# An RWKV block on one core: the bonus term of two groups moved to a ones-block matmul and a channel-major v, and xr's preparation queued behind k's evictions

## The chip, the cores and the metric

The kernel runs on 1 core of one Trainium2 chip, as one program. The metric is device time in microseconds, the median of several runs. Engines: PE is TensorE, DVE is VectorE, ACT is ScalarE, POOL is GpSimd, and SP is the engine that issues most DMAs.

## The reference

Three layers follow one another, for B=2 sequences of S=768 tokens, 8 heads of D=48 channels (384 in all):

```
for t in range(S):                                   # layer 1: linear attention
    cur = einsum('bhd,bhe->bhde', u[None] * kt, vt)  # the bonus of the current token
    y[:, :, t] = einsum('bhd,bhde->bhe', rt, state + cur)
    state = wt[..., None] * state + einsum('bhd,bhe->bhde', kt, vt)
xk = mu_k * x + (1 - mu_k) * x_prev                  # layer 2: x is y, x_prev the token before
xr = mu_r * x + (1 - mu_r) * x_prev
x2 = sigmoid(xr @ w_r) * (relu(xk @ w_k)**2 @ w_v)
h = gelu(x2 @ w_in); u, v = halves of h              # layer 3: gated unit mixing over tokens
out = x2 + (u * (w_sg @ norm(v) + b_sg)) @ w_out
```

The bonus adds, for one token, (sum over d of r_d u_d k_d) times v_e to y_e: one scalar for each token and head, times the head's v.

## The kernel before, in words

Tokens are cut into four groups of 384 (two per sequence), each group into three chunks of 128. The eight heads go in pairs, so a group has four *units* of one pair each, and there are 16 units, 0 to 15. A pair lies on 112 partitions: head 0 on 0 to 47, head 1 on 64 to 111.

A unit runs in four steps. `attn_prep` (DVE) makes decay products by scans, the scaled keys `kp`, the scaled queries `rp`, and `ruk` = r u k. `attn_sc` (step S, line 345) transposes `kp` into PSUM (`kt_ps`, line 351), sums `ruk` over channels by matmuls with the two-column `hm` into the same PSUM tile (`bs`, line 354), has ACT copy the transposed keys out (`kt`, line 357), and forms the scores (`sc`, line 365). DVE then forms `vb` = v times the bonus sums (line 369, v being token-major) and masks the scores (`am`, line 374). `attn_kv` (step K) makes the chunk states. `attn_y` (step Y) collects y for the pair in one PSUM tile: scores times v (line 424), `vb` times the identity (line 427), states times `rp` (line 430); ACT evicts it to `yo` (line 435), and SP copies `yo` by DMA to its place in `xx` (line 444).

Layer 2 runs by group in steps k (8 tiles of 128 rows of `w_k`), r (3) and v (3, each in four parts). `moe1_prep` makes its operand xk or xr from `xx`: for each of three row blocks ACT scales (`dx`, line 484), DVE mixes in the shifted tokens (line 487), and where products are split into a high and a low half, ACT copies the high half (line 490) and DVE subtracts (line 491). A k tile is evicted by ACT (`kr`, line 510). Most products are split: three matmuls in a short fp32 format (`fp32r`) stand for one. The first steps use plain fp32 instead, one matmul that the trace records as two.

The order of PE's instructions is written out by hand: a list of steps in which the attention steps of the next group are woven between the k, r and v steps of the present one, so that units 4 to 7 run beside group 1's layer 2, units 8 to 11 beside group 2's and 12 to 15 beside group 3's. Group 4's layer 2 and then layer 3 follow without attention. The other engines and their DMA queues are ordered by a planner: each operation has a due time (`at(...)`, from the planned start `TS` or end `TE` of a step), and the planner takes, among what is ready in its own model, what is due first. On the chip each queue then runs in that fixed order. `tc.issue_after(ins)` adds that the operations of the block on `ins`'s engine stand behind `ins` in that queue. Tiles of one tag share `bufs` buffers; a new tile waits until the oldest one's readers are done.

xr of group 1 to 4 is prepared once the first k tile of the group has been issued (`if kd == "k" and key[2] == 0`), with due times just ahead of the r step.

Weights come in 64-bit words and are converted on chip (`load64`, lines 225 to 229); a tile tag `wl` with NW1 + SPARE buffers holds full weights, low halves, and pieces of layer 3's weights that are converted ahead.

Of the kernel before, what the change touches and what calls it, by code (L numbers as in the profile page):

```python
# [4 lines left out]
F32 = mybir.dt.float32  # L5
# [3 lines left out]
AF = mybir.ActivationFunctionType  # L9
ALU = mybir.AluOpType  # L10
PSUM = bass.MemoryType.PSUM

B, H, S, D = 2, 8, 768, 48
DM, DFF, DH = 384, 1024, 512
CH = 128
G = 384
GB = S // G
NG = B * GB
CG = G // CH
NP = H // 2  # L20
PW = 2 * D
HP = 64
PR = HP + D
# [5 lines left out]
KS = S // 128  # L29
NTOK = B * S  # L30
NW1 = 2 * KF + KM
SPARE = 4
ND0 = 22
ND = 1
B_STG = 3
# [3 lines left out]
T_GAP = 4.5  # L39
T_TAIL = 9.0  # L40
VQ = 4
L_SPLIT = 2
L_CV = 12
L_CK = 6
# [15 lines left out]
def emit(tc, tin, nin, vt, consts, ucp, mu_k, mu_r, g_ln, b_sg, w_k, w_v, w_r, w_in, w_sgT, w_out, outT):  # L60
# [87 lines left out]
    pl = {"w": tc.alloc_tile_pool(name="pw", bufs=1, side="left", reuse_waits="tile")}  # L148
    pa = tc.alloc_tile_pool(name="pa", bufs=2, side="right", reuse_waits="tile")

    cst = pa.tile([128, 128 + 128 + 2], F32, name="cst", bufs=1)
    ident = cst[:, 0:128]
    cmask = cst[:, 128:256]
    hm = cst[0:PR, 256:258]
    d1f = pa.tile([PR, WL], F32, name="d1f", bufs=1)
    u_sb = pa.tile([PR, NP], F32, name="u_sb", bufs=1)
    flag = cp.tile([1, 1], I32, name="flag")
# [20 lines left out]
    for t in sblk[0] + sblk[1] + scar:  # L178
        PL.memset(t, 0.0)

    uw, urk, uv = {}, {}, {}

    def load_t(i):
        s, hp = divmod(i, NP)
        g, c0, n = subs[s]
        src = tin[g * NP + hp]
        wl = n * (CH + 1) + 1
        w = pa.tile([PR, wl], F32, name="uw", tag="uw", bufs=3)
        rk = pa.tile([PR, 2, n * CH], F32, name="urk", tag="urk", bufs=3)
        e = A if i < 2 else SP  # L190
        with at(TS["S", i] - 9 if i >= 2 else -19.9 + 0.25 * i):
            SP.dma_start(w, src[:, c0 * (CH + 1):c0 * (CH + 1) + wl])
        with at(TS["S", i] - 8.5 if i >= 2 else -19.8 + 0.2 * i):
            e.dma_start(rk, src[:, WL:WL + 2 * G].rearrange("p (q t) -> p q t", q=2)[:, :, c0 * CH:(c0 + n) * CH])
        uw[i], urk[i] = w, rk

    def load_n(i):
# [147 lines left out]
    def attn_sc(i):  # L345
        tS, tK, tY = TS["S", i], TS["K", i], TS["Y", i]
        s = st[i]
        nc_ = subs[i // NP][2]
        kt_ps = pq.tile([128, 512], F32, name="kt_ps", tag="kt", bufs=1)
        for c in range(nc_):  # L350
            PE.transpose(kt_ps[:, c * PR:(c + 1) * PR], s["kp"][:, c], ident[0:PR, 0:PR])
        bs = kt_ps[:, nc_ * PR:nc_ * PR + 2 * nc_]
        for c in range(nc_):
            PE.matmul(bs[:, 2 * c:2 * c + 2], s["ruk"][:, c * CH:(c + 1) * CH], hm, start=True, stop=True)  # L354
        kt = pa.tile([128, nc_, PR], F32, name="kt", tag="ktsb")
        with at(tS + 0.5):
            A.activation(kt, kt_ps[:, 0:nc_ * PR].rearrange("p (c d) -> p c d", d=PR), AF.Copy)
        s["kt"] = kt
        am = pa.tile([128, 2, nc_, CH], F32, name="am", tag="am", bufs=B_AM)
        sc = [pq.tile([128, 512], F32, name="sc", tag="sc", bufs=2)[:, 0:nc_ * CH].rearrange("p (c t) -> p c t", t=CH)  # L360
              for _ in range(2)]
        for c in range(nc_):
            for h in range(2):
                hs = slice(h * HP, h * HP + D)
                PE.matmul(sc[h][:, c], s["kp"][hs, c], s["rp"][hs, c], start=True, stop=True)  # L365
        vb = pa.tile([128, nc_, 2, D], F32, name="vb", tag="vb", bufs=2)
        with at(tY - 1.4):
            bh = bs.rearrange("p (c h) -> p c h", h=2)[:, :, :, None].to_broadcast([128, nc_, 2, D])
            V.tensor_tensor(vb, uv[i].rearrange("p c (h d) -> p c h d", h=2)[:, :, :, 0:D], bh, ALU.mult)
        s["vb"] = vb  # L370
        for h in range(2):
            with at(tY - 1.2 + 0.4 * h):
                mask = cmask[:, None, :].to_broadcast([128, nc_, CH])
                V.tensor_tensor(am[:, h], sc[h], mask, ALU.mult)  # L374
        s["at"] = am
# [39 lines left out]
    def attn_y(i):  # L415
        s = st[i]
        si, hp = divmod(i, NP)
        g, c0, nc_ = subs[si]
        y = pq.tile([128, 512], F32, name="y", tag="y", bufs=1)
        y3 = y[:, 0:nc_ * CH].rearrange("p (c t) -> p c t", t=CH)  # L420
        for c in range(nc_):
            for h in range(2):
                hs = slice(h * HP, (h + 1) * HP if h == 0 else PR)
                PE.matmul(y3[hs, c], uv[i][:, c, hs], s["at"][:, h, c], start=(c == 0), stop=False, skip_group_check=True)  # L424
        for c in range(nc_):
            for h in range(2):
                PE.matmul(y3[h * HP:h * HP + D, c], s["vb"][:, c, h], ident, start=False, stop=False, skip_group_check=True)  # L427
        cs = [c for c in range(nc_) if s["us"][c] is not None]
        for c in cs:
            PE.matmul(y3[0:PR, c], s["us"][c], s["rp"][:, c], start=False, stop=(c == cs[-1]), skip_group_check=True)  # L430
        yo = pa.tile([PR, nc_ * CH], F32, name="yo", tag="yo", bufs=2)
        if hp == 0 and g % GB == 0 and c0 == 0:
            PL.memset(xx[g][:, :, 0:1], 0.0)
        with at(TE["Y", i] - 0.3):
            A.activation(yo, y[0:PR, 0:nc_ * CH], AF.Copy)
        with at(TE["Y", i] - 0.2):
            for h in range(2):
                a = hp * PW + h * D
                e = a + D
                while a < e:  # L440
                    j, p = divmod(a, 128)
                    n = min(e - a, 128 - p)
                    q = h * HP + a - hp * PW - h * D
                    SP.dma_start(xx[g][p:p + n, j, 1 + c0 * CH:1 + (c0 + nc_) * CH], yo[q:q + n])
                    a += n
        if hp == NP - 1 and c0 + nc_ == CG and g % GB != GB - 1:
            with at(TE["Y", i] + 2):
                PL.tensor_copy(xx[g + 1][:, :, 0:1], xx[g][:, :, G:G + 1])
# [20 lines left out]

    m1 = {}  # L470

    def moe1_prep(s, which):
        g, c0, n = subs[s]
        t0, t1 = c0 * CH, (c0 + n) * CH
        x = xx[g]
        mu, nu, nm = ((mk_sb, nk_sb, "xk"), (mr_sb, nr_sb, "xr"))[which]
        nat = is_nat(s, "kr"[which])
        ops = tuple(pl["w"].tile([128, KM, t1 - t0], F32 if nat else F32R, name=nm + q, tag=nm + q, bufs=1)
                    for q in ("h" if nat else "hl"))
        dl = TS[("k", "r")[which], s, 0] - (4 if s == 0 and which == 0 else 0)  # L480
        for j in range(KM):
            d = pl["w"].tile([128, t1 - t0], F32, name="dx", tag="dx", bufs=2)
            with at(dl - 2.5 + 0.5 * j):
                A.activation(d, x[:, j, 1 + t0:1 + t1], AF.Copy, scale=mu[:, j:j + 1])  # L484
            o = ops[0][:, j] if nat else d
            with at(dl - 2 + 0.5 * j):
                last = V.scalar_tensor_tensor(o, x[:, j, t0:t1], nu[:, j:j + 1], d, ALU.mult, ALU.add)  # L487
                if nat:
                    continue
                A.activation(ops[0][:, j], d, AF.Copy)  # L490
                V.tensor_tensor(ops[1][:, j], d, ops[0][:, j].bitcast(F32), ALU.subtract)
        m1[s, which] = ops
        return last

# [8 lines left out]
    def moe1_k(s, f):  # L503
        nat, nt = is_nat(s, "k"), subs[s][2] * CH
        ps = mm_tile()[:, 0:nt]
        mm(ps, [(part(wt["k", f], slice(None), j), part(m1[s, 0], slice(None), j)) for j in range(KM)])
        kr = pl["w"].tile([128, nt], F32, name="kr", tag="kr", bufs=2)
        te, tv = TE["k", s, f], TS["v", s, 0] + f * MM[s, "v"]
        with at(te):
            A.activation(kr, ps, AF.Relu)  # L510
        vn = is_nat(s, "v") and (f < NVN or not split_ops[0])
        kh = pl["w"].tile([128, nt], F32 if vn else F32R, name="kh", tag="kh", bufs=KF)
        dl = min(te + 1, tv - 2)
        if s == NAT["k"] - 1:
            split1("k", f, TS["k", s + 1, f])
        if vn:
            with at(dl):
                A.activation(kh, kr, AF.Square)
            m1[s, "k", f] = (kh,)
            return  # L520
        kl = pl["w"].tile([128, nt], F32R, name="kl", tag="kl", bufs=KF)
        with at(dl):
            A.activation(kh, kr, AF.Square)
            A.activation(kr, kr, AF.Square)  # L524
            V.tensor_tensor(kl, kr, kh.bitcast(F32), ALU.subtract)  # L525
        m1[s, "k", f] = (kh, kl)
# [252 lines left out]
    for n, key in enumerate(keys[:n_in]):  # L779
# [4 lines left out]
        if kd == "Y":  # L784
# [7 lines left out]
            prep(g + 2)  # L792
            if g % NP == NP - 1:
                moe1_prep(g // NP, 0)
        if kd == "k" and key[2] == 0:
            moe1_prep(g, 1)
        if kd == "v" and g == NS - 2 and key[2:] == (KM - 1, VQ - 1):
            pa.release()
            pq.release()
# [78 lines left out]
```

## Time and profile before

| | |
|---|---|
| median of 3 runs | 366.05 us (365.37 to 366.79) |
| profiled execution, its own time | 365.97 us |
| span of its profile | 364.2 us |
| PE, DVE, ACT, POOL busy | 347.2, 249.8, 199.6, 41.2 us |
| instructions | 6202 |

The span is the time from the first to the last instruction on the core. Busy time is a union of an engine's instructions; PE's matmuls overlap each other in the records, so the pitch of matmuls is read from their starts. In a timeline a merged line `x6` covers six records of one kind that follow one another. `[1.36 <-DVE dx L487]` says how long the engine sat idle before the instruction and what released it.

### The profile page before, as it was taken

The numbers are of one execution on the slowest core, as the hardware profiler recorded it, in microseconds if no ns is written. First come the engines' busy times: TensorE is split into PE (matmuls) and PEld (weight loads), VectorE is DVE, ScalarE is ACT, GpSimd is POOL, SyncE is SP. The second block draws the span as 40 slices with busy tenths as digits, with TensorE's granted clock in tenths as the row PEclk, the third lists the DMA queues.
The fourth block names the chain that finished last, engine by engine and source line by source line (L and its number), as shares of the span: only waits on it lengthen the run. The fifth ranks groups of instructions, "written<-read, shape, count | busy, mean of one in ns | idle before, by whom it ended". The sixth has DMA issues, their size and how long they took to land.

```text
span 364.2 us, 6202 instructions
## 1 busy us (share of the span) xinstructions
PE 347.2 (95%) x2281; PEld 297.2 (82%) x2281; DVE 249.8 (69%) x554; ACT 199.6 (55%) x463; POOL 41.2 (11%) x61
## 2 busy tenths in 40 slices
PE   8898699979999999999999999999999999999993
PEld 2686366746666698999999999998899998999992
DVE  6966799999598898655432967469789950835531
ACT  1377668968548875576733899586471315301100
POOL 1000004320292000000000432300000000000000
PEclk9889699999999999999999999999999999999999
DMA  8966577679302542100002141531332001010012
GB/s 197 285 171 175 174 197 206 208 196 245 93 0 61 168 136 61 37 3 16 18 16 61 43 131 52 179 113 39 89 81 59 3 22 45 22 43 2 0 69 72
DMA packets 28775, 34.48 MB, mean 95 GB/s; under 512 B 4032, under 2 KB 25280, under 8 KB 28736
## 3 DMA queue, kind: packets, MB, share of 16 engines
q1 hardware_dynamic: 26336, 30.55, 29.8%
q10 hardware_dynamic: 2400, 3.44, 3.3%
q8 instruction: 20, 0.33, 0.4%
q14 instruction: 19, 0.16, 0.1%
HBM read 29.27 MB, written 2.36 MB: 87 GB/s over the span
## 4 chain that ended last, share of the span: by engine, by line
PE 73%; DVE 9%; DMA 8%; ACT 5%; issue 2%; SPq 1%; ACTq 0%; DVEq 0%
PE mm L468 35%; PE mn L468 26%; DMA xx<-yo 3%; PE sc L365 3%; DMA uw<-tin 3%; PE y L424 2%; PE y L430 2%; PE y L427 2%; PE kt_ps L354 2%; DMA stg<-w_v 1%; DMA stg<-w_r 1%; ACT sblk L411 1%; DVE pf L331 1%; DVE dx L487 1%; DVE pr L335 1%
## 5 line engine op out<-in xcount | busy, mean ns | idle before, releaser
L468 PE MATMUL mm<-xkh,wk 128*128 128x384 f32 x96 | 36.8, 524 | 4.1 <-DVE xkh L487 3.8
L456 ACT ACTIVATE gah<-gt 128x384 fp32r<-128x384 f32 x16 | 8.4, 527 | 43.9 <-DVE gt L620 43.9
L468 PEld LDWEIGHTS mm<-xkh,wk 128*128 128x128 f32 x96 | 18.2, 201 | 16.2 <-DVE xkh L487 5.2
L411 ACT ACTIVATE sblk<-zt,pf 48x48 f32<-48x48 f32 x64 | 21.3, 332 | 4.7 <-DVE zt L400 2.0
L525 DVE TENSOR_TENSOR kl<-kr,kh 128x384 fp32r<-128x384 f32 x24 | 14.4, 605 | 13.0 <-ACT kr L524 12.9
L484 ACT ACTIVATE dx<-xx,par 128x384 f32<-128x384 f32 x24 | 14.3, 613 | 14.4 <-DMA xx<-yo 11.9
L331 DVE TENSOR_TENSOR_SCAN pf<-uw,d1f 112x387 f32<-112x387 f32 x16 | 16.0, 1004 | 8.9 <-ACT scar L411 4.5
L468 PE MATMUL mm<-kh,wvh 128*128 128x384 f32 x64 | 22.0, 344 | 0.0
L225 ACT ACTIVATE stg<-stg 128x384 uint32<-128x384 uint8 x31 | 17.4, 562 | 7.6 <-DMA stg<-w_v 3.1
L468 PE MATMUL mm<-kh,wvl 128*128 128x384 f32 x64 | 21.4, 335 | 0.0
L468 PE MATMUL mm<-kl,wvh 128*128 128x384 f32 x64 | 21.4, 335 | 0.0
L234 POOL TENSOR_TENSOR w2l<-wf,w2h 128x384 fp32r<-128x384 f32 x12 | 13.4, 1124 | 69.2 <-ACT w2h L233 69.2
L468 PE MATMUL mn<-wsh,vl 128*128 128x384 f32 x60 | 20.0, 334 | 0.0
L468 PE MATMUL mn<-wsh,vh 128*128 128x384 f32 x60 | 20.0, 334 | 0.0
L468 PE MATMUL mn<-wsl,vh 128*128 128x384 f32 x60 | 20.0, 334 | 0.0
L510 ACT ACTIVATE kr<-mm 128x384 f32<-128x384 f32 x27 | 13.1, 485 | 10.7 <-PE mm L468 10.1
L487 DVE SCALAR_TENSOR_TENSOR dx<-xx,par,dx 128x384 f32<-128x384 f32 x15 | 12.0, 814 | 8.6 <-ACT dx L484 8.5
L424 PEld LDWEIGHTS y<-am,uv 128*48 128x48 f32 (+1 forms) x192 | 10.7, 134 | 7.9 <-DVE am L374 2.6
L374 DVE TENSOR_TENSOR am<-sc,cst 128x384 f32<-128x384 f32 x32 | 16.8, 551 | 0.0
L424 PE MATMUL y<-am,uv 128*48 128x128 f32 (+1 forms) x192 | 15.0, 289 | 1.7 <-DVE am L374 1.7
L468 PE MATMUL mm<-kh,wv 128*128 128x384 f32 x48 | 16.3, 490 | 0.0
L365 PE MATMUL sc<-rp,kp 48*128 48x128 f32 x192 | 15.7, 299 | 0.0
(200 smaller groups left out, 1015.3 us busy)
## 6 DMA issues: line engine op xcount, KB each, us to landing
urk<-tin SPq DMA_DIRECT2D x14, 336.0 KB, 3.8
stg<-w_k SPq DMA_DIRECT2D x8, 384.0 KB, 4.3
stg<-w_v SPq DMA_DIRECT2D x8, 384.0 KB, 3.4
stg<-w_in SPq DMA_DIRECT2D x8, 384.0 KB, 3.9
uw<-tin SPq DMA_DIRECT2D x16, 169.8 KB, 3.4
uv<-nin ACTq DMA_DIRECT2D x14, 192.0 KB, 3.4
wq<-tin SPq DMA_DIRECT2D x16, 168.0 KB, 2.4
wsf<-w_sgT SPq DMA_DIRECT2D x12, 192.0 KB, 4.7
```

Of the source, the lines that this page charges most:

```text
L225: A.activation(wl, top, AF.Copy, bias=0.5 / 32 - 0.5, scale=1.0 / 32)
L234: e.tensor_tensor(lo, full, hi.bitcast(F32), ALU.subtract)
L331: V.tensor_tensor_scan(pf[:, 0:n1], w[:, 0:n1], d1f[:, 0:n1], 1.0, ALU.mult, ALU.add)
L365: PE.matmul(sc[h][:, c], s["kp"][hs, c], s["rp"][hs, c], start=True, stop=True)
L374: V.tensor_tensor(am[:, h], sc[h], mask, ALU.mult)
L411: A.activation(sb[hs, hs], o[hs], AF.Copy, scale=s["pe"][c][hs])
L424: PE.matmul(y3[hs, c], uv[i][:, c, hs], s["at"][:, h, c], start=(c == 0), stop=False, skip_group_check=True)
L468: PE.matmul(ps, l, r, start=(first and k == 0), stop=(last and k == len(prods) - 1))
L484: A.activation(d, x[:, j, 1 + t0:1 + t1], AF.Copy, scale=mu[:, j:j + 1])
L487: last = V.scalar_tensor_tensor(o, x[:, j, t0:t1], nu[:, j:j + 1], d, ALU.mult, ALU.add)
L510: A.activation(kr, ps, AF.Relu)
L525: V.tensor_tensor(kl, kr, kh.bitcast(F32), ALU.subtract)
```

## The change

For units 8 to 15 (`wide`) the bonus no longer goes through token-major sums. A 112x112 block matrix of ones, `hblk`, comes with the constants; one matmul `hblk` times `ruk` gives in a PSUM tile `ab` the bonus sum of a token on every channel of its head. `ab` takes the single buffer of the tag `kt`, which `kt_ps` uses too. DVE multiplies `ab` by `uvt`, the unit's v in channel-major layout, and writes the product over `ruk`; DVE adds that to y's PSUM tile as it evicts it to `yo`. `uvt` is loaded by SP from a new third part of `tin`, 112 x 384 fp32, into one buffer. The `hm` matmuls, `vb` and its identity matmuls stay for units 0 to 7. `yo` has one buffer instead of two, `SPARE` is 3 instead of 4, and `cst` is 112 columns wider.

xr of groups 2 to 4 is issued after the fourth k tile (index 3) instead of the first, and the ACT scaling of its three row blocks stands behind the `kr` evictions of k tiles 1, 2 and 3 in ACT's queue.

```diff
-SPARE = 4
+SPARE = 3
+N_DIAG = 2
-    cst = pa.tile([128, 128 + 128 + 2], F32, name="cst", bufs=1)
+    cst = pa.tile([128, 258 + PR], F32, name="cst", bufs=1)
+    hblk = cst[0:PR, 258:258 + PR]
+    def wide(i):
+        return i >= NP * N_DIAG
+        if wide(i):
+            uvt[i] = pa.tile([PR, n * CH], F32, name="uvt", tag="uvt", bufs=1)
+            with at(TS["Y", i] - 9):
+                SP.dma_start(uvt[i], src[:, WL + 2 * G + c0 * CH:WL + 2 * G + (c0 + n) * CH])
-        for c in range(nc_):
+        for c in range(0 if wide(i) else nc_):
             PE.matmul(bs[:, 2 * c:2 * c + 2], s["ruk"][:, c * CH:(c + 1) * CH], hm, start=True, stop=True)
+        if wide(i):
+            ab = pq.tile([128, 512], F32, name="ab", tag="kt", bufs=1)[0:PR, 0:nc_ * CH]
+            PE.matmul(ab, hblk, s["ruk"], start=True, stop=True)
+            with at(tY - 1.4):
+                V.tensor_tensor(s["ruk"], ab, uvt[i], ALU.mult)
+            self_am(i, am, sc, tY)
+            return
-        for c in range(nc_):
+        for c in range(0 if wide(i) else nc_):
             for h in range(2):
                 PE.matmul(y3[h * HP:h * HP + D, c], s["vb"][:, c, h], ident, start=False, stop=False, skip_group_check=True)
-        yo = pa.tile([PR, nc_ * CH], F32, name="yo", tag="yo", bufs=2)
+        yo = pa.tile([PR, nc_ * CH], F32, name="yo", tag="yo", bufs=1)
-            A.activation(yo, y[0:PR, 0:nc_ * CH], AF.Copy)
+            if wide(i):
+                V.tensor_tensor(yo, y[0:PR, 0:nc_ * CH], s["ruk"], ALU.add)
+            else:
+                A.activation(yo, y[0:PR, 0:nc_ * CH], AF.Copy)
-    def moe1_prep(s, which):
+    def moe1_prep(s, which, hold=()):
+            if j < len(hold):
+                with tc.issue_after(hold[j]):
+                    last = mix()
+            else:
+                last = mix()
+            if not nat:
+                halves()
-            A.activation(kr, ps, AF.Relu)
+            m1[s, "ev", f] = A.activation(kr, ps, AF.Relu).ins
-        if kd == "k" and key[2] == 0:
-            moe1_prep(g, 1)
+        if kd == "k" and key[2] == (0 if g < 1 else KM):
+            moe1_prep(g, 1, [] if g < 1 else [m1[g, "ev", f] for f in range(1, KM + 1)])
```

`mix()` is the ACT scaling and the DVE mix of one row block, `halves()` the ACT copy and DVE subtraction; `self_am` is the masking of the scores, as before. On the host, `tin` gains `lay_t(inputs["v"], 0.0)` as its last part and `consts` the ones blocks.

## Rows read from the trace of the kernel before

**Rows 1.** Busy us (share of the span) and instructions of each engine, from the page.

```profile
PE 347.2 (95%) x2281; PEld 297.2 (82%) x2281; DVE 249.8 (69%) x554; ACT 199.6 (55%) x463; POOL 41.2 (11%) x61
```

**Rows 2.** PE's busy tenths in 40 equal slices, from the page.

```profile
PE   8898699979999999999999999999999999999993
```

**Rows 3.** Windows: busy us of each engine by stretch, granted clock, DMA share, GB/s.

```profile
0.00:40.00 40.00, 32.92 (x278) 22.57 (x278) 28.56 (x69) 20.01 (x51) 1.82 (x17) 0.90 0.77 204
100.00:156.00 56.00, 55.58 (x409) 44.33 (x408) 46.14 (x91) 36.86 (x86) 11.67 (x11) 1.00 0.26 75
156.00:196.00 40.00, 40.00 (x357) 36.36 (x356) 16.70 (x37) 23.83 (x55) 0.00 (x0) 1.00 0.05 13
196.00:336.00 140.00, 140.00 (x774) 135.71 (x773) 94.94 (x231) 73.17 (x165) 16.30 (x24) 1.00 0.22 64
```

**Rows 4.** Waits over the whole span: who waited for whom, us in total, times, longest.

```profile
POOL w2l L234 <- ACT w2h L233: 69.2, 9, 50.0
...
PE kv L390 <- ACT kt L357: 0.9, 1, 0.9
...
PE mm L468 <- DVE xx L553: 0.3, 1, 0.3
```

**Rows 5.** Timeline of PE from 93.9: start, us, plain fp32 products of layer 2.

```profile
93.94 7.91 PE L468 MATMUL mm<-kh,wv 128*128 128x384 f32 x24
101.69 4.03 PE L468 MATMUL mm<-xkh,wk 128*128 128x384 f32 x12
```

**Rows 6.** Timeline of PE in unit 12, steps S and Y.

```profile
157.07 0.45 PE L351 MATMUL kt_ps<-cst,kp 112*128 112x112 f32 x3
157.36 0.74 PE L354 MATMUL kt_ps<-cst,ru 112*128 112x2 f32 x6
158.03 0.94 PE L365 MATMUL sc<-rp,kp 48*128 48x128 f32 x12
158.90 0.44 PE L468 MATMUL mm<-xkh,wkh 128*128 128x384 f32 x1
...
163.51 0.82 PE L427 MATMUL y<-cst,vb 128*48 128x128 f32 x12
164.26 0.47 PE L430 MATMUL y<-rp,scar 112*112 112x128 f32 x2
```

**Rows 7.** Chain that ended last, one piece: start, us, split products of 384 columns.

```profile
145.78 11.45 PE mm L468 x66
```

**Rows 8.** Timeline of ACT in unit 12's step S.

```profile
157.27 0.49 ACT L510 ACTIVATE kr<-mm 128x384 f32<-128x384 f32 x1
158.13 0.45 ACT L357 ACTIVATE kt<-kt_ps 128x336 f32<-128x336 f32 x1 [0.38 <-PE kt_ps L354]
158.48 0.52 ACT L523 ACTIVATE kh<-kr 128x384 fp32r<-128x384 f32 x1
```

**Rows 9.** Timeline of ACT: y's eviction of unit 3, and group 4's fourth k eviction.

```profile
36.09 0.49 ACT L435 ACTIVATE yo<-y 112x384 f32<-112x384 f32 x1
...
212.62 0.49 ACT L510 ACTIVATE kr<-mm 128x384 f32<-128x384 f32 x1
```

**Rows 10.** Groups by line and shape: busy us, mean ns of one | idle before, releaser.

```profile
L374 DVE TENSOR_TENSOR am<-sc,cst 128x384 f32<-128x384 f32 x32 | 16.8, 551 | 0.0
...
L484 ACT ACTIVATE dx<-xx,par 128x384 f32<-128x384 f32 x24 | 14.3, 613 | 14.4 <-DMA xx<-yo 11.9 <-DVE xrl L491 0.7 <-DVE xkl L491 0.7
...
L369 DVE TENSOR_TENSOR vb<-uv,kt_ps 128x288 f32<-128x288 f32 x16 | 7.2, 451 | 10.9 <-ACT kt L357 10.9
```

**Rows 11.** DMA issues: KB each, median us from issue to landing.

```profile
xx<-yo SPq DMA_DIRECT2D x24, 72.0 KB, 2.2
...
cst<-consts SPq DMA_DIRECT2D x1, 129.0 KB, 4.0
```

**Rows 12.** Timeline of SP's queue: unit 2's y copies.

```profile
32.17 1.78 SPq L444 DMA_DIRECT2D xx<-yo  x3
```

**Rows 13.** Timeline of PE where group 4's r step begins.

```profile
215.51 0.33 PE L468 MATMUL mn<-xrh,wrh 128*128 128x384 f32 x1
```

More of the change, by code (lines that the diff above doesn't have):

```diff
@@ L179, in emit @@
         PL.memset(t, 0.0)
-    uw, urk, uv = {}, {}, {}
+    uw, urk, uv, uvt = {}, {}, {}, {}
+    def wide(i):
+        return i >= NP * N_DIAG
     def load_t(i):
@@ L370, in attn_sc, with self_am @@
         s["vb"] = vb
+        self_am(i, am, sc, tY)
+    def self_am(i, am, sc, tY):
+        s = st[i]
+        nc_ = subs[i // NP][2]
         for h in range(2):
@@ L482, in moe1_prep, with mix, halves @@
             d = pl["w"].tile([128, t1 - t0], F32, name="dx", tag="dx", bufs=2)
[L483 to L491, printed above, removed]
+            def mix():
+                with at(dl - 2.5 + 0.5 * j):
+                    A.activation(d, x[:, j, 1 + t0:1 + t1], AF.Copy, scale=mu[:, j:j + 1])
+                o = ops[0][:, j] if nat else d
+                with at(dl - 2 + 0.5 * j):
+                    return V.scalar_tensor_tensor(o, x[:, j, t0:t1], nu[:, j:j + 1], d, ALU.mult, ALU.add)
+            def halves():
+                with at(dl - 2 + 0.5 * j):
+                    A.activation(ops[0][:, j], d, AF.Copy)
+                    V.tensor_tensor(ops[1][:, j], d, ops[0][:, j].bitcast(F32), ALU.subtract)
+            if j < len(hold):
[5 more added lines that the diff above has]
+                halves()
         m1[s, which] = ops
@@ L846 @@
         lay_t(inputs["k"], 0.0).reshape(NG * NP, PR, G),
+        lay_t(inputs["v"], 0.0).reshape(NG * NP, PR, G),
     ], axis=2)
@@ L854 @@
         ucp[h * HP:h * HP + D] = inputs["u"].reshape(NP, 2, D)[:, h].T
-    consts = np.zeros((128, 258), np.float32)
+    consts = np.zeros((128, 258 + PR), np.float32)
     consts[:, 0:128] = np.eye(128, dtype=np.float32)
@@ L859 @@
         consts[h * HP:h * HP + D, 256 + h] = 1.0
+        consts[h * HP:h * HP + D, 258 + h * HP:258 + h * HP + D] = 1.0
     arrays = {
```

## The prediction

> **What bounds the kernel now.** I read from coarse to fine. The busy shares: TensorE 95% of the span, VectorE 69%, ScalarE 55% [rows 1]. A mean over stages says little, so next the slices of 9.1 us: TensorE has holes up to the ninth, about 82 us, and then nines to the last but one [rows 2]. The windows turn this into stages: PE is idle for 7.1 us in the first 40, for 0.42 us in 100 to 156, and for nothing at all from 156 to 336, all at the 2.4 GHz level (granted clock 1.00) [rows 3]. The wait list says what most of the 0.42 was: one wait of 0.3 us, near 107 us, for VectorE to empty a PSUM tile [rows 4]. So from 100 us on the kernel is bound by TensorE's instruction stream. A microsecond taken out of it there comes off the end, unless another engine now makes it wait; a microsecond taken off another engine there is worth nothing.
>
> The changed units are 8 to 15 (groups 3 and 4), and the first of them starts right behind 12 records of k that begin at 101.69 [rows 5], in the saturated stretch. The PE timeline of unit 12 is the row to argue from [rows 6]. Differences of starts (durations overlap) give 0.29 us for the three transposes, 0.67 for the bonus sums (157.36 to 158.03), 0.87 for the scores, and later 0.75 for the bonus products into y (163.51 to 164.26).
>
> **The change part by part.**
>
> *Bonus on TensorE, removed.* Per wide unit the three `hm` matmuls go (six records, 0.67 us) and the six products of `vb` and the identity (twelve records, 0.75 us): 1.42 us [rows 6], all on the path. Times 8: -11.4 us.
>
> *Bonus on TensorE, added.* One matmul, 112x112 stationary, 384 fp32 columns. Before has none of that shape; nearest is the plain fp32 matmul 128x384, two records each: 24 records run from 93.94 to 101.69, 7.75 us, or 0.646 a matmul [rows 5]. The ends: two records at the pitch of the split format, 66 in 11.45 us or 0.35 for two [rows 7]; and 0.646 with a change of operands that shows, 0.75. I take 0.68, near the row of its own format. Times 8: +5.4. Net of both parts: 0.74 a unit, -5.9 us.
>
> The trace shows an fp32 record every 0.323 us [rows 5]. The Trainium skill, "TensorE: Matmul & The Clock Gate", section "Wait — 56ns, not 53.3ns?", gives a warm start-to-start of columns over 2.4 GHz plus about 2.5 ns; by it two records of 384 are 0.33 us, and the sum would gain 2.8 us more. The trace does not agree for fp32, and the measurement decides.
>
> *A wait added on TensorE.* `ab` uses the single `kt` buffer, so it must wait until ScalarE has copied `kt_ps` out. Before, PE met that copy first at `kv`, behind a whole k, r or v step; now it meets it 0.29 + 0.87 = 1.16 us into the unit. PE is in order, so the step's products and the unit's `kv` queue behind `ab`. When is the copy ready? ScalarE is emptying the k tile just finished (from 157.27, 0.20 into the unit, 0.49 long) and the copy takes 0.45 [rows 8]: 0.20 + 0.49 + 0.45 = 1.14. A dead heat. From below 0 a unit; from above the copy queued behind two more copies of that k step (0.52 each) as well, about 1.0. I take 0.1, since in the row ScalarE stood idle for 0.38 before the copy. Times 8: +0.8.
>
> *VectorE.* The `vb` product (0.45) becomes `ruk` = ab x v, PSUM in, 112x384, priced as the mask product, 0.55; y's eviction (0.49 on ScalarE [rows 9]) becomes an add with PSUM in, 0.55 too [rows 10]. So +0.65 us a unit here. TensorE's stream hides it if VectorE keeps up: in 156 to 196 it is busy 16.7 of 40 us, in 100 to 156 46.1 of 56 [rows 3]. Behind an add that waits for y queue the next units' scans and kl; behind a `ruk` product that waits for v's DMA queue the mask products, which PE needs. Lost cover comes under rival 1; here 0.2 in all, between 0 and 2.6 (4 x 0.65).
>
> *xr held behind k's evictions (groups 2 to 4).* In group 2 VectorE can then empty earlier the PSUM tile that cost PE 0.3 us [rows 4]: -0.3, between 0 and -0.42 [rows 3]. In groups 3 and 4 PE does not wait there, so nothing is won. Moved are three ScalarE scalings, three VectorE mixes, three copies and three subtractions; no DMA. They are due when r starts.
>
> *Loads.* `uvt` adds 172 KB on SP's queue for each of eight units. Its buffer is freed at the unit's `ruk` product, a unit ahead of the next use, and DMA is 5% busy in 156 to 196, 26% in 100 to 156 [rows 3]: 0, at most one landing delay of 4.0 us, as `cst` had it, in one unit [rows 11]. `cst` grows by 57 KB in the opening, which waits for loads: at the 204 GB/s of that stretch 0.28 us [rows 3], by the transfer's own 129 KB in 4.0 us 1.8 [rows 11], from below 0. I take 0.25.
>
> *Buffers.* With one y buffer an eviction waits for the previous unit's DMAs. Tightest is the opening: three issues over 1.78 us from 32.17, the last near 33.4, landing 2.2 later, before the eviction at 36.09 [rows 9, 11, 12]: 0, at most 0.5. With one spare weight tile fewer, three w_in pieces instead of four are converted early; such a piece waited up to 50 us for its place [rows 4]: 0, at most one ScalarE pass, 0.6 [rows 10].
>
> The sum, against the profiled execution (span 364.2, 365.97 with what lies around it): -11.4 + 5.4 + 0.8 + 0.2 - 0.3 + 0.25 = -5.0, so 361.0 us. The median of the runs shown, 366.05, is the same within 0.1.
>
> **The rivals.**
>
> *1. VectorE falls behind in group 3.* To the 46.1 of 56 us [rows 3] come 4 x 0.65 = 2.6, and the stretch shrinks by 4 x 0.74 = 3.0: 48.7 of 53, 92%; xr's work moves into its fullest part. If in each of the four units one such operation, 0.55 to 0.65, stands ahead of a mask product that PE waits for, 4 x 0.6 = 2.4: 363.4. For it: that load. Against: PE had no wait for a mask product after 100 us, and the conversions of w_in mixed in there can slip to after 156.
>
> *2. Slower: ScalarE's copy comes late at every* `ab`. If ScalarE's order puts the whole k eviction (0.49 and two copies of 0.52) and one held scaling (0.61) ahead of the kt copy [rows 8, 10], that ends 0.20 + 2.14 + 0.45 = 2.8 us into the unit, 1.63 after the scores: 8 x (1.63 - 0.74) = +7.1, so 373. It decides from a mean wait of 0.74 us on. For it: PE did meet a late kt copy once even at `kv`, 0.9 us [rows 4]. Against: in rows 8 the copy ran before the k step's other two, with ScalarE waiting for its input.
>
> *3. xr comes late for r in group 4.* There k's fourth eviction was at 212.62 and r began at 215.51 [rows 9, 13]; scaling 0.61, mix and subtraction 0.6 each and a copy 0.52 take 2.3 for the last third. If ScalarE's backlog puts four more operations of 0.5 in front, r waits about 2 us: 363.0.
>
> *4. The bonus matmul runs at the split format's pitch,* 0.35: 8 x 0.33 = 2.6 less, 358.4. Rows 5 speak against it. The section of the Trainium skill named above speaks for it.
>
> That the bonus was hidden anyway needs PE slack from 105 to 195, which rows 3 exclude; it has no chance of its own.
>
> **How the numbers follow.** Forecast 0.62, rival 1 0.16, rival 2 0.09, rival 3 0.09, rival 4 0.04. The forecast alone spans 359.4 (no wait at `ab`, nothing on VectorE or for loads, 0.65 a matmul) to 362.6 (0.3 a unit at `ab`). The range goes from there, 359.3, to 364.6, rival 1 with another 0.15 lost at each `ab`; it leaves out rivals 2 and 4 and the worst of the loads. About 0.5%, 1.8 us, is what a measurement of this kernel can tell from no change. Faster, below 364.2: the forecast bar 0.02, rivals 3 and 4, two thirds of rival 1 and a little less, 0.83. Same 0.10: the rest of rival 1 and mild forms of rival 2. Slower 0.07, its full form.
>
> **What would show it.** The bonus-sum records halve from 96 to 48, those of `vb` from 192 to 96, and sixteen `ab` records appear, in steps of 0.65 to 0.75 a unit. PE stays without holes from 100 us to the end of the last product, and waits for the kt copy before `ab` sum to about 1 us. Group 4's k step begins about 5 us earlier. It is wrong if PE's waits for mask products or kt add to over 4 us after 100 us, if `ab` takes well under 0.5, or if the opening grows by over 1 us.

## The result, and the profile after

The changed kernel takes 371.45 us (median of 4 runs, 368.87 to 372.67) where the kernel before takes 366.42 beside it (4 runs): a ratio of 1.0124, 95% interval 1.0089 to 1.0158. It is slower by some 4.5 us by the ratio (5.0 between the medians); forecast were 361.0 and at most 364.6. The profiled execution took 371.91 us, with a span of 370.1. Of the runs below, e5 alone had executions over 1.5% above its fastest, three of twelve: its ratio leaves them out, its median of 365.75 does not.

TensorE's row and slices of the page, in answer to [rows 1, 2]:

```profile
PE 345.2 (93%) x2153; PEld 290.7 (79%) x2153; DVE 253.1 (68%) x562; ACT 193.0 (52%) x455; POOL 41.9 (11%) x61
...
PE   7799399968999999999999989999999999999993
```

PE's busy time fell by only 2.0 us while the span grew by 5.9: most of the work that left came back as holes, or as products at the lower clock. The slices say where: a 3 in the fifth (37 to 46 us; 6 before), an 8 in the 24th (213 to 222). The windows of [rows 3], columns as there:

```profile
0.00:40.00 40.00, 32.70 (x278) 22.91 (x278) 27.49 (x67) 19.48 (x50) 2.01 (x16) 0.87 0.80 213
100.00:156.00 56.00, 54.10 (x336) 38.96 (x335) 41.86 (x86) 30.47 (x74) 13.46 (x14) 1.00 0.29 83
156.00:196.00 40.00, 39.78 (x304) 34.51 (x303) 22.56 (x48) 24.39 (x58) 0.00 (x0) 1.00 0.10 26
196.00:336.00 140.00, 138.47 (x752) 132.95 (x752) 94.13 (x228) 72.74 (x165) 17.59 (x24) 0.99 0.23 67
```

Idle in 100 to 156 went from 0.42 to 1.9 us, and the stretch from 196 on, which had none, now has 1.5 us and a granted clock below 1.00. TensorE's own waits over the span (total, times, longest):

```profile
PE mm L492 <- DVE xkh L513: 5.8, 2, 4.5
PE kv L411 <- ACT kt L366: 5.0, 2, 2.6
PE y L451 <- ACT sblk L432: 3.2, 9, 0.9
...
PE mn L492 <- ACT xrh L517: 1.2, 2, 0.8
...
PE ab L377 <- ACT kt L366: 0.4, 2, 0.2
```

The first two are the opening (before 3.8 and 0.9). 1.7 of the 3.2 us for `sblk` (ScalarE's copies of the chunk states, which the last products of step Y read), and all for `xrh` (the high half of xr), lie after 100 us, where before had neither. `ab` waits for 0.4 us in all.

Landmarks read from the starts in TensorE's timelines put this together, in us. *The hold* is the second part of the change: xr issued after the fourth k tile, its scalings queued behind k's evictions. The kernels e1 to e16 and b_yo1 are described in the next section. Each row is one profiled execution; executions of one kernel differ by 2 to 6 us (after and e16: 2.4 of it before unit 8, 1.5 in r). The first column above all is rough: up to 78 us e9 runs every engine in the order of the kernel before, and yet TensorE is 0.8 us later there, and 1.7 at unit 8. So what a part costs is read from the ratios, and where it is lost from the rows.

| kernel | unit 8 starts | units 8 to 11 | unit 12 to group 4's k | group 4's r |
|---|---|---|---|---|
| before | 105.56 | 51.51 | 45.96 | 4.68 |
| after | 109.86 | 51.29 | 43.71 | 8.76 |
| e16, after again | 107.45 | 51.10 | 43.70 | 7.29 |
| e9, no bonus | 107.28 | 49.07 | 41.00 | 4.68 |
| e1, no hold | 110.66 | 50.80 | 43.43 | 4.68 |
| e2, hold alone | 105.10 | 51.81 | 45.96 | 10.84 |
| e15, after with `ab` behind kv | 109.35 | 49.95 | 43.45 | 8.87 |
| e3, no hold in group 4 | 108.55 | 51.11 | 43.73 | 4.68 |
| b_yo1, one yo buffer alone | 108.22 | 50.69 | 45.96 | 4.68 |
| e13, two yo buffers | 106.30 | 51.51 | 43.73 | 8.76 |
| e14, small constants | 108.97 | 50.23 | 43.73 | 7.30 |
| e10, both | 105.72 | 52.86 | 43.73 | 7.29 |
| e5, no hold, two yo buffers | 106.97 | 54.70 | 43.43 | 4.68 |
| e6, no hold, two yo buffers, small constants | 105.44 | 51.80 | 43.42 | 4.68 |
| e8, e6 with the hold in groups 2, 3 | 105.48 | 51.11 | 43.72 | 4.68 |
| e7, e6 with ab behind kv | 105.62 | 50.44 | 43.45 | 4.68 |
| e11, e7 with group 2 wide | 106.37 | 51.23 | 43.46 | 4.68 |
| e12, e7 with group 4 alone wide | 104.98 | 51.36 | 43.45 | 4.68 |

The rest, from group 4's v to the last product, is 137.86 us before and after. So of the 5.9 us by which the last product came later in these two executions, 4.3 are there before the first wide unit begins and 4.1 are r's in group 4; the wide units gave back 2.5, nearly all of it in group 4.

### The profile page after: what moved, and what is told of

Its sections match the earlier page's. It is cut to its first block, busy times and chain, and to the rows that moved or that the text cites. A ratio compares the mean times of both kernels' runs of the same rounds, so it can differ in the third digit from the quotient of the medians.

```text
span 370.1 us, 5946 instructions
## 1 busy us (share of the span) xinstructions
PE 345.2 (93%) x2153; PEld 290.7 (79%) x2153; DVE 253.1 (68%) x562; ACT 193.0 (52%) x455; POOL 41.9 (11%) x61
## 4 chain that ended last, share of the span: by engine, by line
PE 62%; DVE 16%; ACT 9%; DMA 6%; issue 3%; SPq 1%; ACTq 0%; POOL 0%; DVEq 0%
PE mm L492 29%; PE mn L492 24%; DMA xx<-yo 3%; DVE pf L340 2%; PE sc L374 2%; DVE pr L344 2%; PE y L445 2%; PE y L451 2%; ACT kr L545 1%; ACT sblk L432 1%; DMA stg<-w_k 1%; DMA uw<-tin 1%; DMA stg<-w_v 1%; PE ab L377 1%; SPq L468 1%
## 5 line engine op out<-in xcount | busy, mean ns | idle before, releaser
L492 PE MATMUL mm<-xkh,wk 128*128 128x384 f32 x96 | 35.7, 512 | 5.8 <-DVE xkh L513 5.8
L243 POOL TENSOR_TENSOR w2l<-wf,w2h 128x384 fp32r<-128x384 f32 x12 | 14.7, 1237 | 68.9 <-ACT w2h L242 68.9
L340 DVE TENSOR_TENSOR_SCAN pf<-uw,d1f 112x387 f32<-112x387 f32 x16 | 16.8, 1047 | 5.6 <-DMA uw<-tin 3.4
L344 DVE TENSOR_TENSOR_SCAN pr<-uw,d1r 112x387 f32<-112x387 f32 x16 | 15.3, 958 | 0.2
L451 PE MATMUL y<-rp,sblk 112*112 112x128 f32 x64 | 12.4, 304 | 3.2 <-ACT sblk L432 3.2
```

The costliest lines, as they stand in the source:

```text
L243: e.tensor_tensor(lo, full, hi.bitcast(F32), ALU.subtract)
L340: V.tensor_tensor_scan(pf[:, 0:n1], w[:, 0:n1], d1f[:, 0:n1], 1.0, ALU.mult, ALU.add)
L344: V.tensor_tensor_scan(pr[:, 1:wl][:, ::-1], w[:, 1:wl][:, ::-1], dr[:, 1:wl][:, ::-1], 0.0, ALU.mult, ALU.add)
L492: PE.matmul(ps, l, r, start=(first and k == 0), stop=(last and k == len(prods) - 1))
```

## The experiments

Times of different chips are compared by their ratio to the kernel before on the same chip; 0.01 is 3.7 us. Each run of this section had 6 to 12 executions.

**e16: the changed kernel again.** 

> The changed kernel once more, unaltered, as the measure for the three runs beside it: 1.009 to 1.016 of the kernel before by its first measurement. If it came out at 1.005 or less, the first runs of it were late by chance, and part of the 5 us that the experiments explain would not be there.

369.94 us, ratio 1.0126 (1.0094 to 1.0159): the loss is there again.

**e9: what the removed part was worth.**

```diff
-        for c in range(nc_):
+        for c in range(nc_ if i < 8 else 0):
             PE.matmul(bs[:, 2 * c:2 * c + 2], ...
```

and likewise `vb` and its products; the bonus of units 8 to 15 is left out. 

> The kernel before with the bonus left out of units 8 to 15 (its small matmuls, the product on DVE and the six adds into y); everything else as before. It measures the term that the prediction took off in full. Theory A (1.42 us of a unit, all on PE's path): from the first unit of group 3 to k of group 4, 97.5 us before, becomes 86 to 87, and the time 354.5 to 355.5. Rival B (the other engines fill part of the room: group 3 is held by ACT or DVE): 89 to 92 us, time 358 to 361, with waits of PE for ACT or DVE in group 3.

360.12 us, ratio 0.9823 (0.9773 to 0.9873): 6.5 us, not 11.4. Unit 12 in steps S and Y, in TensorE's timeline of this kernel, and below it step S of the changed kernel:

```profile
156.35 0.45 PE L351 MATMUL kt_ps<-cst,kp 112*128 112x112 f32 x3
156.73 0.94 PE L365 MATMUL sc<-rp,kp 48*128 48x128 f32 x12
157.60 0.45 PE L469 MATMUL mm<-xkh,wkh 128*128 128x384 f32 x1
...
161.54 0.87 PE L425 MATMUL y<-am,uv 128*64 128x128 f32 x12
162.34 0.47 PE L431 MATMUL y<-rp,scar 112*112 112x128 f32 x2
```

```profile
161.15 0.45 PE L360 MATMUL kt_ps<-cst,kp 112*128 112x112 f32 x3
161.53 0.94 PE L374 MATMUL sc<-rp,kp 48*128 48x128 f32 x12
162.40 0.90 PE L377 MATMUL ab<-ru,cst 112*112 112x384 f32 x2
162.84 0.63 PE L492 MATMUL mm<-xkh,wkh 128*128 128x384 f32 x1
```

The transposes now take 0.38 from start to start instead of 0.29, and the products of scores and v 0.80 instead of 0.70 (in the trace of before they start at 162.81, and `vb`'s at 163.51 [rows 6]): what stands in front of the next operation grew. In the single records the last product before the scores starts 0.18 or 0.19 us ahead of them in both kernels, and the last one before the states 0.20, while their like follow each other at about 0.10: this step from one kind of product to the next stays, whichever product stands ahead of it. Why it takes longer is not shown. From unit 12 to 13 it is 8.30 us here and 9.54 before, 1.24 a unit and not 1.42. With `ab` a unit is 8.92 (e7), so `ab` costs 0.62. Group 4 gave the 1.24 four times, 4.96; group 3 only 2.44, since PE waits there 1.5 us for `sblk` and 0.6 for DVE's emptying of a PSUM tile. Rival B, in the size and in the waits.

**e1, e2, e3: the hold.** The edit of e1, all groups; e3 does it in group 4 alone; e2 puts the hold into the kernel before:

```diff
-        if kd == "k" and key[2] == (0 if g < 1 else KM):
-            moe1_prep(g, 1, [] if g < 1 else [m1[g, "ev", f] for f in range(1, KM + 1)])
+        if kd == "k" and key[2] == 0:
+            moe1_prep(g, 1)
```

> The changed kernel with one part undone: the inputs of r are made when k starts, in all groups, as before. Theory A (the hold makes r of the last group late: 8.76 us from k's to v's start of r's steps instead of 4.68, the clock's fall in it included): about 4 us less than the changed kernel, near 367.4, with r of the last group back at 4.7 us and no fall of the granted clock there. Rival B (r is late because the wide units end sooner and leave ACT more behind, whatever the hold): r of the last group still takes over 7 us and the time stays near 371. Both leave the first unit of group 3 some 4 us late, at 110 us.

> The kernel before with the held inputs of r alone; bonus, loads and buffers as before. Theory A: the hold by itself costs r of the last group 3 to 4 us (it takes 7.7 to 8.8 us where before took 4.68) and may give 0.3 us in group 2, so 369 to 370.5. Rival B (the hold hurts only beside the wide units): within 1 us of the kernel before, 365.5 to 367.5, r of the last group at 4.7 to 5.2 us.

> The changed kernel with one edit: the hold of r's inputs is undone in group 4 alone. Theory A (the hold pays in group 3, where it keeps ACT's copy of kt early, and costs only in group 4): below the kernel with no hold at all (366.7), 364 to 366.5, so 5 to 7 us below the changed kernel; r of the last group 4.7 us. Rival B (the hold costs in groups 2 and 3 as well, by PE's waits for sblk): above the kernel with no hold, 367.5 to 369.

e1: 366.67 us, 1.0011 (0.9984 to 1.0039), 4.2 us below the changed kernel (e16's ratio); r is back at 4.68, with no fall of the clock: theory A. e2: 373.66, 1.0204 (1.0172 to 1.0236): the hold by itself costs 7.5 us, more than either theory gave it, and 6.2 of it are r's in its profiled execution. e3: 367.42, 1.0051 (1.0025 to 1.0077): undone in group 4 alone it returns 2.7 us, with r at 4.68. Theory A is wrong here: e3 is not faster than e1 but 1.5 us slower by the ratios, whose intervals meet, just under the range of rival B. So no gain of the hold in groups 2 and 3 shows with one yo buffer; with two, e8 below shows one.

TensorE at r in the changed kernel, the windows of that stretch (columns as in [rows 3]), and ScalarE ahead of it:

```profile
217.34 0.33 PE L492 MATMUL mn<-xrh,wrh 128*128 128x384 f32 x1
...
218.87 0.45 PE L492 MATMUL mn<-xrh,wrh 128*128 128x384 f32 x1 [0.84 <-ACT xrh L517]
...
220.49 0.51 PE L492 MATMUL mn<-xrh,wrh 128*128 128x384 f32 x1 [0.41 <-ACT xrh L517]
...
222.90 0.53 PE L492 MATMUL mn<-xrh,wrh 128*128 128x384 f32 x1
...
226.10 0.33 PE L492 MATMUL mm<-kh,wvh 128*128 128x384 f32 x1
```

```profile
217.30:218.80 1.50, 0.73 (x5) 0.41 (x3) 1.09 (x2) 1.50 (x5) 0.00 (x0) 1.00 0.00 0
218.80:220.50 1.70, 1.08 (x4) 0.50 (x4) 1.01 (x2) 1.70 (x6) 0.00 (x0) 1.00 0.00 0
220.50:222.00 1.50, 1.36 (x4) 1.04 (x5) 0.91 (x3) 1.50 (x4) 0.00 (x0) 0.57 0.00 0
222.00:224.00 2.00, 2.00 (x8) 2.00 (x7) 0.79 (x2) 1.41 (x4) 0.00 (x0) 0.50 0.00 0
224.00:226.00 2.00, 2.00 (x13) 2.00 (x12) 0.32 (x1) 1.29 (x4) 0.00 (x0) 0.97 0.00 0
```

```profile
214.88 0.61 ACT L510 ACTIVATE dx<-xx,par 128x384 f32<-128x384 f32 x1
...
217.00 0.61 ACT L510 ACTIVATE dx<-xx,par 128x384 f32<-128x384 f32 x1
...
217.93 0.48 ACT L545 ACTIVATE kr<-mn 128x384 f32<-128x384 f32 x1
218.30 0.52 ACT L517 ACTIVATE xrh<-dx 128x384 fp32r<-128x384 f32 x1
...
219.91 0.52 ACT L517 ACTIVATE xrh<-dx 128x384 fp32r<-128x384 f32 x1
```

The k step gives ScalarE one eviction and two copies for every nine products of 1.56 us. By their durations these take 1.5 us; but ScalarE's records overlap, and from start to start they take 1.2 (215.80 to 217.00). Each third of xr adds a scaling and a copy, 0.5 and 0.4 from start to start, so a tile with both takes 2.1, and from 212.5 to 222 ScalarE is never free. Each held scaling stands in that queue behind k's work, so the last copy of xr ends at 220.43, 3.1 us after r's first product. Then the clock falls to the 1.2 GHz level, with PE busy for 1.81 of the 3.2 us before, and 0.32 us instead of 0.17 lie between starts for some 3 us.

How much of it is the clock? The changed kernel's other profiled execution (e16) has nearly the same waits and no fall (last line: a window, with PE's busy time, granted clock, DMA share and GB/s):

```profile
214.73 0.33 PE L492 MATMUL mn<-xrh,wrh 128*128 128x384 f32 x1
...
216.18 0.44 PE L492 MATMUL mn<-xrh,wrh 128*128 128x384 f32 x1 [0.76 <-ACT xrh L517]
...
217.79 0.44 PE L492 MATMUL mn<-xrh,wrh 128*128 128x384 f32 x1 [0.41 <-ACT xrh L517]
...
222.02 0.33 PE L492 MATMUL mm<-kh,wvh 128*128 128x384 f32 x1
...
218.00:220.00 2.00, 1.79 (x10) 1.00 0.00 0
```

7.29 us against 8.76: the late xr costs 2.6 us over the 4.68 of before, and the clock 1.5 more in the executions in which it falls. e13 and e15 have the fall too, e10 and e14 do not, and their r in the table falls into the same two sizes.

**b_yo1, e13, e14, e10: the late opening.** b_yo1 is the kernel before with one line changed; e13 undoes that line in the changed kernel (channel-major v then uses the buffers of `vb`, and its loads are issued a unit ahead); e14 fills the block of ones on the chip; e10 does both.

```diff
-        yo = pa.tile([PR, nc_ * CH], F32, name="yo", tag="yo", bufs=2)
+        yo = pa.tile([PR, nc_ * CH], F32, name="yo", tag="yo", bufs=1)
```

> The kernel before with one number changed: the tile of y's eviction (yo) has one buffer instead of two. Theory A (that buffer is what makes the opening late: an eviction waits for the transfer of the one before it, and the order written for ACT and SP changes with it from unit 3 on): the first unit of group 3 starts 2.5 to 3.5 us later than in the kernel before (108 to 109 us instead of 105.6) and the time is 368.5 to 370. Rival B (the loads made it late: constants of 185 KB instead of 129, longer rows of the input): the first unit of group 3 stays at 105.6 and the time at 366.4.

> The changed kernel with two yo buffers alone (channel-major v in the buffers of vb); constants of 185 KB, hold and ab as changed. Theory A (the single buffer makes the opening late): 1.001 to 1.005 of the kernel before, 2.5 to 4 us below the changed kernel, with the first unit of group 3 at 106.5 to 107.5 us. Rival B (the larger constants do): 1.009 to 1.012, first unit of group 3 at 109.

> The changed kernel with the block of ones filled on the chip alone, so constants of 129 KB; one yo buffer, hold and ab as changed. Theory A (the constants cost 1 to 1.5 us at most): 1.008 to 1.011 of the kernel before, first unit of group 3 at 108 to 109. Rival B (they cost the larger part of the 4.4 us): 1.001 to 1.004, first unit of group 3 at 106.

> The changed kernel with two yo buffers again (channel-major v in the buffers of vb) and the block of ones filled on the chip; hold in groups 2 to 4 and everything else as changed. It measures what the buffer and the larger constants cost in the changed kernel itself. Theory A (the opening's 4.3 us come from these two, the buffer most): first unit of group 3 at 105.3 to 106, time 368 to 369.5. Rival B (they cost it only in single runs): 370.5 to 371.5.

b_yo1: 368.4 us, 1.0069 (1.004 to 1.0098), unit 8 at 108.22: the buffer alone costs 2.5 us. e13: 366.69, 1.0016 (0.9987 to 1.0044): 4.0 us back. e14: 368.9, 1.0105 (1.0071 to 1.014): 0.8 us, not told from nothing. e10: 366.39, 1.0004 (0.998 to 1.0028): 4.5 us back, more than expected. By b_yo1 it is the buffer, theory A. But e13 and e10 change one thing more than the buffer. The first load of channel-major v stands in the opening of the changed kernel, and in e13 it does not:

```profile
26.10 0.42 SPq L203 DMA_DIRECT2D uvt<-tin  x1
```

```profile
88.79 0.38 SPq L209 DMA_DIRECT2D uvt<-tin  x1
```

So of the 4.0 us 2.5 are the buffer's by b_yo1, and how the other 1.5 are shared between it and this load is not shown. In e16, with the load at 24.71, TensorE's starts up to 36 us are within 0.7 us of those in the kernel before, earlier or later; in the first profile of the changed kernel they are up to 1.5 us later.

How, the kernel before and b_yo1 show, at the first k tile of group 1: before first, ScalarE and TensorE; then the same in b_yo1.

```profile
36.09 0.49 ACT L435 ACTIVATE yo<-y 112x384 f32<-112x384 f32 x1
...
37.30 0.55 ACT L225 ACTIVATE stg<-stg 128x384 uint32<-128x384 uint8 x1
...
39.62 1.12 ACT L484 ACTIVATE dx<-xx,par 128x384 f32<-128x384 f32 x2 [1.34 <-DMA xx<-yo]
...
40.94 5.04 PE L468 MATMUL mm<-xkh,wk 128*128 128x384 f32 x8 [1.95 <-DVE xkh L487]
```

```profile
36.21 0.47 ACT L435 ACTIVATE yo<-y 112x384 f32<-112x384 f32 x1
37.95 0.54 ACT L225 ACTIVATE stg<-stg 128x384 uint32<-128x384 uint8 x1 [1.28 <-DMA stg<-w_k]
...
39.23 0.55 ACT L225 ACTIVATE stg<-stg 128x384 uint32<-128x384 uint8 x1 [0.30 <-DMA stg<-w_k]
...
40.12 1.10 ACT L484 ACTIVATE dx<-xx,par 128x384 f32<-128x384 f32 x2
...
41.98 5.49 PE L468 MATMUL mm<-xkh,wk 128*128 128x384 f32 x8 [4.06 <-DVE xkh L487]
```

The eviction itself is hardly late, 36.21 instead of 36.09 (the one before it waits for the buffer and starts at 32.03 instead of 31.65, which is made up by 35 us). But the planner models the single buffer, and writes another order for ScalarE, VectorE and SP: two conversions of `w_k`, waiting for loads, now stand between the first scaling and the other two, where one stood before, and VectorE has the second half of one conversion more ahead of its mix. TensorE's wait grows from 1.95 to 4.06 us (4.46 in the changed kernel, where ScalarE also begins later). As its products before the wait began 0.9 us earlier, 1.0 of that is lost; by 46 us it is 1.5. Another 1.3 us is lost near 76 us, at a `kv` that waits for ScalarE's copy of kt. Before first, then b_yo1:

```profile
72.51 0.44 ACT L357 ACTIVATE kt<-kt_ps 128x336 f32<-128x336 f32 x1
...
73.33 0.43 PE L390 MATMUL kv<-uv,kt 128*64 128x48 f32 x8
```

```profile
73.18 1.33 ACT L233 ACTIVATE wvh<-wv 128x384 fp32r<-128x384 f32 x3
...
75.64 0.43 ACT L357 ACTIVATE kt<-kt_ps 128x336 f32<-128x336 f32 x1
...
76.12 0.43 PE L390 MATMUL kv<-uv,kt 128*64 128x48 f32 x8 [0.93 <-ACT kt L357]
```

Between y's eviction and the copy of kt ScalarE now makes three copies of weights (`wvh`), and one in the kernel before. The changed kernel has these three as well, and a wait of 2.56 us behind them; e13 has the one again.

**e5, e6, e8, e7, e15: where `ab` stands.** e5 is e1 with two yo buffers, e6 adds the block filled on the chip, e8 adds the hold in groups 2 and 3 to e6; e7 moves `ab` in e6, e15 in the changed kernel:

```diff
 def attn_sc(i):
-            ab = pq.tile([128, 512], F32, name="ab", tag="kt", bufs=1)[0:PR, 0:nc_ * CH]
-            PE.matmul(ab, hblk, s["ruk"], start=True, stop=True)
...
 def attn_kv(i):                      # after the kv products
+        if wide(i):
+            ab = pq.tile([128, 512], F32, name="ab", tag="kt", bufs=1)[0:PR, 0:nc_ * CH]
+            PE.matmul(ab, hblk, s["ruk"], start=True, stop=True)
```

> The changed kernel with the hold undone, and with two yo buffers again; the room is found by letting the channel-major v use the buffers of the bonus product (vb), which the wide units don't need. Constants and loads stay as changed. Theory A (hold 4 us, one yo buffer 2.5 to 3.5 us): 364 to 365, with the first unit of group 3 at 106.5 to 107.5. Rival B (the opening is late by the loads): 367 to 367.5, first unit of group 3 at 109.5 to 110.

> The kernel of the run before this (hold undone, two yo buffers), and the block of ones is now filled on the chip instead of loaded, so that the constants are 129 KB again; the input's longer rows and the channel-major v's loads stay. Theory A (the larger constants are what is left of the late opening): the first unit of group 3 starts at 105.5 to 106 us instead of 107, and the time falls from 365.75 by 1 to 1.5, to 364.5. Rival B (the longer rows, or nothing that lasts): unit 0 and the first unit of group 3 stay as they were, 365 to 366.

> As the run with the constants back at 129 KB, with the hold of r's inputs in groups 2 and 3 alone, and ab where the change put it. Theory A (in group 3 the hold takes ab's wait of 3 us away and puts 1.7 us of waits for ACT's sblk in its place; group 4 keeps r at 4.7 us): group 3's four units 50.5 to 51.5 us, with ab's waits under 0.5 us, and 362.5 to 364. Rival B (the hold's waits are as long as the one it removes): no better than without it, 364 to 365.

> As the run with the constants back at 129 KB, and the bonus matmul (ab) is moved from the end of the scores to just after the kv products of the same unit, which wait for ACT's copy of kt anyway. Theory A (without the hold, ab's wait for that copy costs 3.4 us in group 3, and the clock falls behind it): group 3's four units take 48.5 to 49.5 us (before 51.5), no wait at ab, and the time is 360.5 to 361.5. Rival B (the wait moves to kv, with the same length): units of group 3 at 51 to 52 us, 364 to 365.

> The changed kernel with ab moved behind kv alone; hold, one yo buffer and constants as changed. Theory A (with the hold ab hardly waits, 0.4 us in the trace, and PE's waits for sblk come from the hold): within 1 us of the changed kernel, 1.010 to 1.014 of the kernel before. Rival B (ab at the end of the scores costs more than its own wait, since it ends late what follows it): 1.005 to 1.009.

e5: 365.75 us, 0.9966 (0.9938 to 0.9995), nearer to theory A. e6: 366.21, 1.0009 (0.9981 to 1.0036), rival B: the constants gave nothing that lasts (its profiled execution was the fastest of twelve). Both lose in group 3 what the wide units give. From e6's list of TensorE's waits after 100 us:

```profile
PE ab L384 <- ACT kt L373: 2.5, 2, 2.3
```

Without the hold, a copy of xr that waits 1.9 us for VectorE's mix, and behind it an eviction and two copies of k and the next eviction, stand ahead of the kt copy in unit 8 (106.18 to 108.47). e8: 363.66, 0.9926 (0.9892 to 0.9961): 0.4 at `ab`, and 1.6 us of waits for `sblk` in its place; theory A, and 3.0 us below e6. e7: 362.33, 0.9879 (0.9838 to 0.992): no wait at `ab`, 4.8 us below e6. Its units of group 3 take 50.44 us, between the two forecasts. The waits at `ab` in e6's trace are only 2.5 us; but that execution had a granted clock of 0.974, and the eleven others, at 0.963 to 0.970, took 1.8 to 5.0 us longer. e7's six had 0.973 to 0.980. So a lower clock goes with a part of the 4.8 us; whether it fell behind these waits no trace shows. e15: 368.7, 1.0078 (1.0049 to 1.0108), 1.8 us below the changed kernel, in the range of rival B, though the two intervals meet; TensorE's waits for `sblk` after 100 us are 1.1 us there, and 1.9 in e16.

**e11, e12: how many groups.** `N_DIAG` 1 and 3 instead of 2 in e7.

> As the run with ab moved behind kv (362.3), and units 4 to 7 (group 2) take the ones-block matmul too. By the measured price of a unit (1.24 us removed, 0.62 added) group 2 would give 2.5 us at most, 360 to 361; by the other theory group 2 is held by ACT's and DVE's conversions of weights and its inputs, PE has waits there already, and the room only lengthens these: 361.5 to 363, or more if the earlier loads of channel-major v delay the weights.

> As the run with ab moved behind kv (362.3), but only units 12 to 15 (group 4) take the ones-block matmul; group 3 has the bonus as before. Theory A (group 3's units gave only about 1.1 us, since PE waits there for other engines): 363.2 to 364. Rival B (group 3 gave as much as group 4, 2.5 us): 364.6 to 365.4.

e11: 363.39, 0.9927 (0.9901 to 0.9953), no gain, the other theory. In group 2 TensorE waits for ScalarE anyway (the whole span):

```profile
PE kv L416 <- ACT kt L373: 5.3, 3, 3.0
```

(3.0 in e7; between 45 and 106 us, beside group 2's units, 3.8 and 1.9). e12: 362.79, 0.9908 (0.9879 to 0.9937): group 3 is worth about 1 us by the ratios, whose intervals meet, and 0.9 by its units' 50.44 against 51.36 us. That is theory A's price, though the median lies 0.4 us under its range.

**The sum.** Ratios in a chain from the kernel before to the changed one: wide units with `ab` behind kv, with one spare weight tile fewer and no hold, 0.9879 (-4.4 us); `ab` at the scores with the hold in groups 2 and 3, 0.9926 (+1.7); the hold in group 4 too, 1.0004 (+2.9); one yo buffer, the larger constants and the early first load of channel-major v, 1.0126 (+4.5). The first, third and fourth step are larger than their intervals. Other chains share it out differently: e6 and e1 differ by the buffer, the constants and that load as well, and by 0.0002 only. Why the late opening costs next to nothing when there is no hold stays open (a lower clock in e6, whose median over its executions is 0.969 where e1 has 0.973, may hide a part).

**e7 beats both kernels:** 1.2% below the one before.

## Why the prediction was wrong

The steps that failed are *Buffers* ("0, at most 0.5") and *xr held behind k's evictions* (nothing lost in groups 3 and 4, with rival 3 as the loss at a chance of 0.09).

- *Bonus removed*, -11.4: 1.24 a unit instead of 1.42, -9.9 if all of it counts (e9). I took differences of starts as prices, and the neighbour ahead grew by 0.09 and 0.10. Of it only 6.5 us came off the time. That the stretch was saturated was right; that it would stay so with 1.24 us less per unit held for group 4, not for group 3.
- *Bonus added*, +5.4: 0.62 a unit, +5.0. Right, and rival 4 falls with it. The Trainium skill, "TensorE: Matmul & The Clock Gate", section "Wait — 56ns, not 53.3ns?", gives, by an estimate from it, about 0.33 for two such records; the trace does not agree for fp32.
- *The wait at `ab`*, +0.8: 0.4 with the hold; without it 2.5 (e6). Rival 2 was wrong for the changed kernel, and right as a mechanism once the hold was gone: the place of `ab` was a real price, most of which the hold covered.
- *VectorE*, +0.2: no wait for `am` or `ru` after 100 us. The two operations took 549 and 559 ns, as priced. Rival 1 is wrong as to who was late: it was ScalarE's `sblk`, 1.7 us.
- *The hold*, -0.3: the 0.3 us wait near 107 us is gone, as forecast. The loss was rival 3, with its mechanism, ScalarE's backlog in group 4: 2.6 us for its 2.0 (its own terms give 2.3 + 2.0 - 2.9 = 1.4), and 1.5 from the clock that it left out. The mistake was to say that xr is "due when r starts" without counting the queue that it was moved behind. From the fourth eviction to r there were 2.9 us [rows 9, 13]; that tile's own two copies of 0.52, the scaling, the mix and the last copy fill 2.8 of it, and the evictions and copies of the four tiles behind it, 1.2 us each from start to start, share the same engine. With that sum rival 3 could not have had a chance of 0.09.
- *Loads*, +0.25: 0.8 for the constants, not told from nothing (e14); `cst` took 5.0 us to land instead of 4.0, `uvt` 2.3. The sum has the opening pay for `cst` alone; the first `uvt` load was issued there too, at 26.10, and its price is not known.
- *Buffers*, 0 to 0.5: 2.5 us in the kernel before (b_yo1), and up to 4.0 in the changed one, the place of the first `uvt` load included (e13). I asked whether the eviction would wait on the chip, and it hardly does. What I left out is that the planner counts the buffer too and writes another order for ScalarE, VectorE and SP. The Trainium skill, "Trainium Kernel Development and Optimization", section "Best Practices", has the rule to double-buffer for performance, so that DMA and compute overlap; b_yo1 agrees that the second buffer is worth having, though what was lost here was lost by the order and not by that overlap. The spare weight tile was not tried alone.

One reading of the rows was off without consequence: not all stretches were at the 2.4 GHz level, the first 40 us had a granted clock of 0.90 [rows 3]. Of the signs named, the record counts (48, 96 and 16) and `ab`'s price came out as forecast. PE's stream without holes after 100 us did not, nor did group 4's k step 5 us earlier (204.86, before 203.03), and the opening grew by more than the 1 us named as a refutation.

## What to carry to other kernels

Where a planner writes the order of an engine, a buffer count or a moved operation is priced by the order that it gives, not by whether the one tile waits. When work is moved behind a queue, count what that queue holds between there and the deadline. A wait put on the bounding engine belongs behind one that it must make anyway: `ab` behind kv kept the gain. And a landmark or a wait from one execution tells where time is lost, not how much: for that take many executions, here 6 to 12.

## What the runs showed of the hardware

Six profiled executions of kernels with wide units and the hold in group 4 have nearly the same holes at r: 0.76 to 0.84 us, then 0.40 or 0.41, and in all but the changed kernel's first another of 0.21, with the granted clock at 1.00 up to there (in the changed kernel PE was busy for 1.81 of 3.2 us). In three (the changed kernel, e13, e15) the clock then fell to 0.50 and r took 8.76 to 8.87 us; in three (e16, e10, e14) it stayed at 1.00 and r took 7.29 or 7.30. That is 1.5 us of difference between executions, and the changed kernel and e16 are the same kernel.

The clock also splits the executions of one kernel. Of e8's twelve, six with a granted clock of 0.977 to 0.979 took 361.75 to 363.49 us, and six with 0.967 to 0.972 took 363.82 to 366.54.
